# Mamba-2 scan and SwiGLU block on one core: row sums kept once with a negated selector, dummy products in five steps, roundings on other engines, and a new order of all steps

## The chip, the cores and the metric

The kernel runs on one core of a Trainium2 chip. A core has five instruction queues that work side by side: PE (matrix products, with PEld for the load of its weights), DVE (vector), ACT (activation functions), POOL (general) and SP, which here issues nearly all DMAs. The metric is the time of one execution on the device in microseconds (us). The runs of the kernel before gave 358.74 (median of three; 358.64, 358.74 and 359.39).

## The reference, cut to what matters

Two stages follow each other. The first is a Mamba-2 scan over 4 batches x 8 heads, 768 positions, 32 columns of x and 16 states, in chunks of 32. Its result, 3072 tokens x 256, goes through a SwiGLU block with 1536 hidden columns.

```python
log_a = np.log(np.clip(a, 1e-06, 1.0))
for c in range(nc):
    cum = np.cumsum(la, axis=-1)
    L = np.exp(cum[:, :, :, None] - cum[:, :, None, :]) * causal
    M = np.einsum('bhin,bhjn->bhij', Cc, Bc) * L
    y_intra = np.einsum('bhij,bhjd->bhid', M, xc)
    y_inter = np.einsum('bhin,bhnd->bhid', Cc, state) * np.exp(cum)[:, :, :, None]
    y[:, :, sl] = y_intra + y_inter
    Bx = np.einsum('bhjn,bhjd->bhjnd', Bc, xc) * np.exp(cum[:, :, -1:] - cum)[..., None, None]
    state = np.exp(np.sum(la, axis=-1))[:, :, None, None] * state + np.sum(Bx, axis=2)
...
x = attn_out.transpose(0, 2, 1, 3).reshape(B * S, H * D)
rms = np.sqrt(np.mean(x * x, axis=-1, keepdims=True) + 1e-06)
xn = x / rms * rms_g
g = xn @ w_gate
silu = g * (1.0 / (1.0 + np.exp(-g)))
return (silu * (xn @ w_val) @ w_out)
```

## The kernel before, in words

**Stages.** The 3072 tokens are six blocks of 512, and each block is two pairs of 256 tokens (pairs 0 to 11). A pair goes through the scan with chunks of 64 or 128 positions instead of 32; a finished block is normed and goes through the SwiGLU products. Block 0 has to pass the scan before any large product can run, so the start of the kernel is the scan of pairs 0 and 1 together with what must be set up for it. Later the scan of a block is interleaved with the products of the blocks before it.

**Large products.** A step `X.block.f.m` (`gv_split`, L1173) makes one 128 x 512 tile of the gate (m = 0) or the value (m = 1) for hidden columns f, as six products of 128 x 512: the operands are split into a high, a low and a mixed part (`xh`, `xl`, `xk` against `wh` and `wp`). `OX` (`o_split`, L1242 and L1248) multiplies the hidden parts `hh`, `hl`, `hk` with the output weights; `OY` (`product_apart`, L1220) does so for the last block; `F` (L1163) and `OF` are the same products with whole operands. The parts are made by ACT, DVE or POOL: `hH` is the rounding to the high part on ACT, `hHv` the same on DVE, `hL` and `hLp` the low part on DVE and on POOL (L1094), `xH`, `xL`, `xK` and `wH`, `wL`, `wM` likewise for the inputs and the weights. A letter p or v at the end of a step's name says that POOL or DVE does it.

**The start.** `a` comes in by a DMA and is turned by PE (`aT`, L454), clipped on DVE (`la0`, L465), and ACT takes its log (`la`). From it PE makes the chunk sums `c` (`chunk_sums`, L570 and L572), other sums `d` (L552 and L555) and, for the pairs 0 and 1, the row sums `r.0`, for the pairs 2 and 3 `r.1` (`sums_of_logs`, L525). `r.k` multiplies the logs with `mids`, a matrix of two halves: `mid` (a triangle about the middle, on POOL) and its negative (`minus_mid`, L485). DVE splits the result into three bf16 parts (`three_parts`, L536 to L541) and puts them into one tile `row` of 128 x 256, positive half and negative half. Then `mask.p.half` writes the causal mask into a bank of PSUM (L608, two products `whole16` x `ident16`), `sums.p.half` adds to it `row` against a selector `sel` (L622, eight small products) and `sel` against the negative half of `row` (L629, two products), and `exp` (ACT) makes the decays `L` of it. Before `r.1`, the step `middles` changes `mid` for chunks of 64 (POOL, L433 and L436, and again `minus_mid`). Other steps there: `turn.p` turns B and C of a pair (L704), `g` multiplies them (L771), `last` and `A`, `y` finish the pairs; `pow`, `man`, `wt` prepare the bf16 parts of the weights; `cx` and `cc` make `early` (ACT and POOL) and its column sums `fcol` (`chunk_column`, L586). `hmask`, `upto`, `after`, `never`, `ident`, `part`, `head`, `sel`, `mean` are constants that POOL and DVE make.

**Dummy products.** `warm` is a tile of zeros. `idle.n` (L447) multiplies it n times with itself into a bank that nobody reads, and `c*2` puts two such products (`filled`, L131) into the bank of `c` ahead of its real ones.

**What sets the order.** The order of the work is a text of steps, written out by hand, that the kernel walks through; there is no scheduler. Each engine executes its own instructions in the order in which the steps issue them. `i:` steps are kinds of the start, `p:` steps take a pair, `b:` steps a block. Banks of PSUM and places of SBUF are handed out by rings, first freed, first used, so the order also says which buffer a step gets. Every DMA goes out in this order from SP's queue, apart from half of the loads of the first pair, which go from ACT's; `fetch.k` loads piece k of the weights (511.5 KB), `bc.p` and `x.p` load B, C and x of a pair.

Of the kernel before, what the change touches and what calls it, by code (L numbers as in the profile page):

```python
# [9 lines left out]
FP32 = mybir.dt.float32  # L10
# [40 lines left out]
def kernel(  # L51
# [12 lines left out]
    nc = tc.nc  # L64
# [302 lines left out]
    mids = lead.tile([P, 2, P], FP32, name="mids")  # L367
# [10 lines left out]
    sel = const.tile([P, NH], BF16, name="sel")  # L378
    kinks = const.tile([P, 3], FP32, name="kinks")
# [6 lines left out]
    mid = mids[:, 0]  # L386
# [45 lines left out]
    def from_middles():  # L432
        nc.gpsimd.tensor_copy(out=mid, in_=upto)  # L433
        for r in halves:
            half_of = slice(r.start, r.start + HC // 2)
            nc.gpsimd.tensor_scalar(out=mid[half_of, r], in0=mid[half_of, r], scalar1=-1.0,  # L436
                                    scalar2=None, op0=ALU.add)
        minus_mid()
# [45 lines left out]
    def minus_mid():  # L484
        nc.gpsimd.tensor_scalar(out=mids[:, 1], in0=mid, scalar1=-1.0, scalar2=None,  # L485
                                op0=ALU.mult)

# [16 lines left out]
                                               op0=ALU.mult),  # L504
        "mid": from_middle, "middles": from_middles,
# [7 lines left out]
        "log": logs, "mids": minus_mid,  # L513
# [9 lines left out]
    def sums_of_logs(k):  # L523
        ps["r", k] = b, r_ps = bank((P, 2, P), 1, "r")
        nc.tensor.matmul(out=r_ps.rearrange("p s m -> p (s m)"),  # L525
                         lhsT=la4[k].rearrange("p q k h -> p (q k h)"),
                         rhs=mids.rearrange("p s m -> p (s m)"), start=True, stop=True)

    def three_parts(k):
        b, r_ps = ps.pop(("r", k))  # L530
        t = h.take(1, "parts")
        both = view(t, [P, 4, P], FP32)
        first = both[:, 0].bitcast(BF16).rearrange("p (s m) -> p s m", s=2)
        second = both[:, 1].bitcast(BF16).rearrange("p (s m) -> p s m", s=2)
        rest = both[:, 2:4]
# [4 lines left out]
        rows[k] = row = const.tile([P, 2, P], BF16, name="row%d" % k)  # L540
# [71 lines left out]
    def sums(p, half, e):  # L612
# [6 lines left out]
        for k, hd in enumerate(heads):  # L619
            for i, r in enumerate(rows_of):  # L620
                for u in parts:
                    nc.tensor.matmul(out=e[i][u, k * n:(k + 1) * n],  # L622
                                     lhsT=sel[r, hd:hd + 1].to_broadcast([32, n]),
                                     rhs=row[r, 0, u], start=p >= 2 and k == 0, stop=False,
                                     tile_position=(r.start, u.start), skip_group_check=True)
        hs = slice(heads[0], heads[-1] + 1)
        for i, r in enumerate(rows_of):
            for u in parts:
                nc.tensor.matmul(out=e[i][u], lhsT=row[r, 1, u],  # L629
                                 rhs=sel[r, hs].unsqueeze(2).to_broadcast([32, len(heads), n]),  # L630
# [714 lines left out]
    def token_out():  # L1345
# [82 lines left out]
        i:sums.1.1 i:exp.0.1 i:fetch.6 i:g.0.1 i:exp.1.1 i:sums.0.0 p:scale.1 p:Tt.1.1 i:last.1
        p:scale.0 p:T.1 i:r.1 i:g.0.0 i:exp.0.0 i:L.0.1 i:tok i:Tl.1 i:g.1.1 i:pow.2 i:mask.1.0
        i:parts.1 i:L.0.0 i:last.0 i:sums.1.0 i:A.1 i:exp.1.0 i:row.1 i:A.0 i:L.1.1 i:g.1.0 i:Tl.0  # L1430
        p:S.0 i:tokout p:bc.2 i:pow.0 i:fetch.1 i:y.0 i:rowe.1 p:bc.3 i:sq.0 i:row.0 i:limit i:L.1.0
        i:sums.3 p:S.1 i:man.0 i:pow.6 i:y.1 i:wt.0 i:rowout.1 i:yt.0 p:dT.2 i:fetch.4 p:turn.2
        i:sq.1 i:yt.1 i:early.0.0 i:open i:man.6 i:wt.6 i:man.1 i:fetch.5 i:man.2 i:exp.3 b:ms.0
        i:rowe.0 i:cav.3 i:early.0.1 i:pow.1 i:sums.2 i:wHv.6 i:wt.1 b:rs.0 i:wt.2 i:fetch.3 p:x.2
        p:dT.3 p:x.3 i:fetch.12 i:fetch.8 p:T.2 i:xn i:exp.2 p:Tt.2.1 p:turn.3 p:Td.2 i:early.1.0
        i:norm.0 p:Tt.2.0 p:T.3 p:Tt.3.1 i:wHv.2 i:rowout.0 i:man.4 i:early.1.1 b:F.0.2.0 i:pow.4
        p:scale.3 i:wt.4 p:Tt.3.0 i:norm.1 b:xH.0.1 i:pow.5 i:ca.2 b:gb.1 i:wL.6 b:L.1.1 b:F.0.4.0
        i:fetch.10 p:scalep.2 b:xH.0.0 b:silu.0.2 i:silu.0 b:xLp.0.1 i:pow.3 b:L.1.3 p:Td.3
        b:F.0.3.0 b:L.1.2 b:L.1.0 b:xK.0.1 b:xK.0.0 i:wHv.1 i:mana.3 b:xLp.0.0 p:A.2 p:S.2 p:A.3
        i:wt.3 b:silu.0.4 i:man.5 i:pow.12 b:F.0.5.0 i:wMp.6 b:X.0.7.0 b:X.0.6.0 i:wHv.3 p:S.3  # L1440
        p:qb.5 b:silu.0.5 i:wL.3 b:silu.0.3 i:fetch.9 i:pow.8 i:man.12 i:fetch.11 p:yi.2 i:wt.5
        p:ya.2 i:pow.10 b:silu.0.6 i:wM.3 p:yi.3 p:ya.3 i:fetch.13 i:wHv.5 b:sq.1.0 i:hid.0 i:wt.12
        p:qc.5 i:wL.5 b:X.0.2.1 i:silu.1 b:yt.1.1 i:mana.10 b:hid.0.2 i:gains i:mana.8 p:vB.5
        i:wMp.5 b:silu.0.7 i:wt.10 b:sq.1.1 b:X.0.3.1 i:fetch.7 i:wt.8 i:pow.13 i:man.13 b:yt.1.0
# [144 lines left out]
```

## Time and profile before

| what | value |
|---|---|
| time, median of three runs | 358.74 us (358.64 to 359.39) |
| span of the profiled execution, first to last instruction | 357.0 us |
| PE busy | 352.7 us (99%) |
| DVE busy | 283.5 us (79%) |
| ACT busy | 196.6 us (55%) |
| POOL busy | 91.1 us (26%) |
| mean granted clock of PE | 0.999 |

The profile gives the profiled execution's span only, not its own time; between the span and the median of the runs lie 1.74 us (358.74 - 357.0), which I take for what lies around the span. Rows of the timeline give start, duration, engine, line and tile; in square brackets stand idle time ahead of the first instruction and what ended it. Rows of the chain follow the end of the kernel back to its start, in order of time. Two instructions of PE can overlap, since it is pipelined: their starts tell more than their durations.

### The profile page before, as it was taken

How to read it: one execution, taken by the hardware profiler on the slowest of the kernel's cores; microseconds unless marked ns; L12 is line 12 of the kernel's file. 1: busy time of each engine (PE TensorE's matmuls, PEld its weight loads, DVE VectorE, ACT ScalarE, POOL GpSimd, SP SyncE). 2: the span in 40 equal slices, each digit the busy share in tenths (PEclk: the TensorE clock that was granted, in tenths of full speed). 3: DMA queues.
4: the chain of work that ended last, by engine and by line, in shares of the span. 5: the costliest groups of instructions: out<-in, count | busy, mean ns of one | idle time of the engine just before them, and what ended most of it. 6: DMA issues, size and time to landing. Idle time of an engine off the chain costs nothing.

```text
span 357.0 us, 8314 instructions
## 1 busy us (share of the span) xinstructions
PE 352.7 (99%) x3329; PEld 285.0 (80%) x3329; DVE 283.5 (79%) x507; ACT 196.6 (55%) x338; POOL 91.1 (26%) x91
## 2 busy tenths in 40 slices
PE   8999999999999999999999999999999999999996
PEld 5677578887888878878788788788788888888896
DVE  6899999999998999987887955877357582875791
ACT  3888999994756757494154672463345342112510
POOL 4125314256211326540123320025101111311000
PEclk9999999999999999999999999999999999999999
DMA  8978986672261345443123011200010021001003
GB/s 105 213 124 242 281 233 189 176 162 51 42 155 55 96 81 136 80 76 75 31 64 102 8 31 29 48 14 2 7 31 0 1 37 23 0 0 31 0 2 88
DMA packets 94556, 27.88 MB, mean 78 GB/s; under 512 B 77463, under 2 KB 92471, under 8 KB 94519
## 3 DMA queue, kind: packets, MB, share of 16 engines
q1 hardware_dynamic: 92438, 27.23, 33.4%
q8 instruction: 26, 0.43, 0.5%
q10 hardware_dynamic: 2080, 0.13, 0.4%
q14 instruction: 12, 0.09, 0.1%
HBM read 23.68 MB, written 3.67 MB: 77 GB/s over the span
## 4 chain that ended last, share of the span: by engine, by line
PE 98%; DVE 1%; issue 0%
PE gv L1173 53%; PE o L1242 19%; PE o L1248 8%; PE y L929 3%; PE o L1220 2%; PE gv L1163 2%; PE gv L1126 2%; PE g L778 2%; PE A L843 1%; PE g L771 1%; PE e L608 1%; PE y L904 1%; PE e L622 1%; PE ms L1027 0%; PE idle L447 0%; PE row L1311 0%
## 5 line engine op out<-in xcount | busy, mean ns | idle before, releaser
L1173 PE MATMUL gv<-xh,wh 128*128 128x512 f32 x272 | 87.0, 401 | 0.0
L272 ACT ACTIVATE hx<-gv 128x512 f32<-128x512 f32 x70 | 40.2, 595 | 80.2 <-PE gv L1173 36.7
L1173 PE MATMUL gv<-xl,wp 128*128 128x512 f32 x272 | 84.1, 390 | 0.0
L1173 PE MATMUL gv<-xk,wp 128*128 128x512 f32 x272 | 83.8, 390 | 0.0
L1096 DVE SCALAR_TENSOR_TENSOR hk<-hx,hh 128x512 fp32r<-128x512 f32 x65 | 53.0, 827 | 25.4 <-PE o L1242 18.9
L1094 POOL TENSOR_TENSOR hl<-hx,hh 128x512 fp32r<-128x512 f32 x21 | 29.7, 1418 | 131.1 <-DVE hk L1096 30.4
L1173 PEld LDWEIGHTS gv<-xl,wp 128*128 128x128 f32 x272 | 51.1, 188 | 11.0
L1173 PEld LDWEIGHTS gv<-xk,wp 128*128 128x128 f32 x272 | 51.1, 188 | 10.9
L1173 PEld LDWEIGHTS gv<-xh,wh 128*128 128x128 f32 x272 | 50.0, 188 | 10.8 <-issue 0.6
L1188 DVE SCALAR_TENSOR_TENSOR hx<-gv,hx 128x512 f32<-128x512 f32 x70 | 47.0, 684 | 13.4 <-PE gv L1173 12.4
L341 ACT ACTIVATE hh<-hx 128x512 fp32r<-128x512 f32 x37 | 22.8, 629 | 39.8 <-PE o L1242 11.9
L1242 PE MATMUL o<-hh,wh 128*128 128x512 f32 x96 | 37.9, 395 | 0.0
L1242 PE MATMUL o<-hl,wp 128*128 128x512 f32 x96 | 37.4, 390 | 0.0
L1242 PE MATMUL o<-hk,wp 128*128 128x512 f32 x96 | 37.4, 390 | 0.0
L1094 DVE TENSOR_TENSOR hl<-hx,hh 128x512 fp32r<-128x512 f32 x44 | 31.1, 721 | 2.8 <-PE o L1242 1.3
L266 ACT ACT_TABLE_LOAD x17 | 21.8, 1283 | 1.1 <-PEq L1573 0.8
L264 ACT ACT_TABLE_LOAD x17 | 21.8, 1283 | 0.3
L1242 PEld LDWEIGHTS o<-hh,wh 128*128 128x128 f32 x96 | 18.0, 188 | 4.2 <-issue 0.4
L336 POOL TENSOR_TENSOR wp<-wh,wp 128x512 fp32r<-128x512 f32 x9 | 13.0, 1449 | 32.6 <-DVE wp L328 25.0
L1242 PEld LDWEIGHTS o<-hk,wp 128*128 128x128 f32 x96 | 18.0, 188 | 3.8
L1242 PEld LDWEIGHTS o<-hl,wp 128*128 128x128 f32 x96 | 18.0, 188 | 3.6
L328 DVE SCALAR_TENSOR_TENSOR wp<-wh,w 128x512 fp32r<-128x512 f32 x27 | 19.6, 751 | 0.0
(184 smaller groups left out, 548.2 us busy)
## 6 DMA issues: line engine op xcount, KB each, us to landing
L<-rowd SPq DMA_DIRECT2D x32, 128.0 KB
x<-in_x_dram SPq DMA_DIRECT2D x24, 128.0 KB
wr<-in_moe_w_out_dram SPq DMA_DIRECT2D x6, 511.5 KB
wr<-in_moe_w_gate_dram SPq DMA_DIRECT2D x5, 511.5 KB
wr<-in_moe_w_val_dram SPq DMA_DIRECT2D x5, 511.5 KB
out_dram<-ob SPq DMA_DIRECT2D x28, 64.0 KB
bc<-in_B_dram SPq DMA_DIRECT2D x23, 64.0 KB
bc<-in_C_dram SPq DMA_DIRECT2D x23, 64.0 KB
```

Source lines behind the costliest of these rows:

```text
L264: nc.scalar.preload_act_table(AF.Silu)
L266: nc.scalar.preload_act_table_set("natural_log_exp_and_others")
L272: nc.scalar.activation(**operands)
L328: nc.vector.scalar_tensor_tensor(out=(low_parts, mixed_parts)[i][k], in0=high_parts[k], scalar=(-UP, GAIN)[i], in1=view(ws[k], shape), op0 ...
L336: nc.gpsimd.tensor_tensor(out=mixed_parts[k], in0=high_parts[k], in1=low_parts[k], op=ALU.subtract)
L341: nc.scalar.activation(out=out, in_=in_, func=AF.Copy, scale=scale)
L1094: engine.tensor_tensor(out=out, in0=v, in1=high, op=ALU.subtract)
L1096: nc.vector.scalar_tensor_tensor(out=out, in0=v, scalar=REST, in1=high, op0=ALU.mult, op1=ALU.subtract)
L1173: nc.tensor.matmul(out=o, lhsT=weights_of(m, t, f)[part], rhs=view(x, [P, TB], F32R), start=(part == t == 0), stop=(part == 2 and t == 1))
L1188: nc.vector.scalar_tensor_tensor(out=v, in0=o, scalar=gain(blk, f), in1=v, op0=ALU.mult, op1=ALU.mult)
L1242: nc.tensor.matmul(out=o, lhsT=w[:, b * P:(b + 1) * P], rhs=v, start=opens, stop=True, skip_group_check=True)
L1248: nc.tensor.matmul(out=o[:, j * DM:(j + 1) * DM], lhsT=v[:, tk], rhs=w, start=opens, stop=True, skip_group_check=True)
```

## The change

1. `mids` of 128 x 2 x 128 becomes `mid` of 128 x 128; the step that made its negative half is gone. `r.k` has 128 columns instead of 256, the split into three parts works on half the width, and `row` is 128 x 128. The second half of each sum takes the minus sign from a new constant, `minus` = -`sel` (128 x 8 bf16, DVE).
2. `fcol` is no longer one reduction on DVE but three additions on POOL, of widths 4, 2 and 1.
3. Dummy products: `idle.7` and `c*2` become `idle.2`, `idle.2`, `idle.2`, `idle.1`, `idle.1` and `idle.1`: nine before and nine after. `idle.2` stands ahead of `aT`, five dummies between `aT` and `c`, one behind `r.0`, one between two masks.
4. Roundings and others change engines. Counted over the text: `hH` on ACT 37 to 30, `hHv` on DVE 28 to 35; `hL` on DVE 44 to 40, `hLp` on POOL 21 to 25; parts of the weights on POOL 9 to 7 and on DVE 27 to 29; `Td` on DVE 8 to 4, on POOL 2 to 6; the scalings of pairs 0 and 1 go to POOL, subtractions on POOL go from 5 to 8.
5. All steps stand in a new order.

```diff
-    mids = lead.tile([P, 2, P], FP32, name="mids")
+    mid = lead.tile([P, P], FP32, name="mid")
...
+    minus = const.tile([P, NH], BF16, name="minus")
...
-        minus_mid()
...
+        "minus": lambda: nc.vector.tensor_scalar(out=minus, in0=sel, scalar1=-1.0, scalar2=None,
+                                                 op0=ALU.mult),
...
-        ps["r", k] = b, r_ps = bank((P, 2, P), 1, "r")
-        nc.tensor.matmul(out=r_ps.rearrange("p s m -> p (s m)"),
-                         lhsT=la4[k].rearrange("p q k h -> p (q k h)"),
-                         rhs=mids.rearrange("p s m -> p (s m)"), start=True, stop=True)
+        ps["r", k] = b, r_ps = bank((P, P), 1, "r")
+        nc.tensor.matmul(out=r_ps, lhsT=la4[k].rearrange("p q k h -> p (q k h)"), rhs=mid,
+                         start=True, stop=True)
...
-        rows[k] = row = const.tile([P, 2, P], BF16, name="row%d" % k)
+        rows[k] = row = const.tile([P, P], BF16, name="row%d" % k)
...
-        nc.vector.reduce_sum(out=fcol, in_=ps["fsel"], axis=AX.X)
+        rest = ps["fsel"]
+        for w in (4, 2, 1):
+            out = fcol.unsqueeze(2) if w == 1 else ps["full"][:, :, 4 - w:4]
+            nc.gpsimd.tensor_tensor(out=out, in0=rest[:, :, 0:w], in1=rest[:, :, w:2 * w],
+                                    op=ALU.add)
+            rest = out
...
-                                     rhs=row[r, 0, u], start=p >= 2 and k == 0, stop=False,
+                                     rhs=row[r, u], start=p >= 2 and k == 0, stop=False,
...
-                nc.tensor.matmul(out=e[i][u], lhsT=row[r, 1, u],
-                                 rhs=sel[r, hs].unsqueeze(2).to_broadcast([32, len(heads), n]),
+                nc.tensor.matmul(out=e[i][u], lhsT=row[r, u],
+                                 rhs=minus[r, hs].unsqueeze(2).to_broadcast([32, len(heads), n]),
...
-        i:warm i:a i:set i:bc.0 i:ident i:bc.1 i:bc2.1.1 i:ones i:zeros i:ident16 i:whole i:kinks
-        i:idle.7 i:after i:never i:fetch.2 i:whole16 i:mean i:part i:head i:part2 i:sel i:after2
...
+        i:ones i:hmask i:upto i:ident i:part i:warm i:idle.2 i:zeros i:a i:fetch.2 i:whole i:aT
+        i:la0 i:bc.0 i:mid i:idle.2 i:head i:set i:idle.2 i:log i:log4.0.4 i:idle.1 i:tmask
```

What the new order does to DVE and POOL at the very start. DVE before:

```order
L489 MEMSET warm 128x128
L494 MEMSET ones 128x128
L495 MEMSET never 128x128
L506 CAST ident_81<-ident 128x128
L403 MEMSET chunk_ones 128x256
L405 MEMSET chunk_ones 64x128 x2
```

and after:

```order
L489 MEMSET ones 128x128
L415 TENSOR_REDUCE part<-ident 128x4
L484 MEMSET warm 128x128
L490 MEMSET never 128x128
L403 MEMSET chunk_ones 128x256
L405 MEMSET chunk_ones 64x128 x2
L464 TENSOR_SCALAR early<-aT 128x64x3
```

`warm` was DVE's first instruction and is now behind `part`, which reads `ident`. POOL's, which makes `ident`, before:

```order
masks.py:197 MEMSET ident 128x128
masks.py:199 ISA
masks.py:199 AFFINE_SELECT ident<-ident 128x128
L399 AFFINE_SELECT after<-ones 128x128
L399 AFFINE_SELECT never<-never 128x128
L399 AFFINE_SELECT upto<-ones 128x128
```

and after:

```order
L408 ISA
L408 AFFINE_SELECT hmask<-ones 128x8
L410 AFFINE_SELECT hmask<-hmask 128x8
L399 AFFINE_SELECT upto<-ones 128x128
masks.py:197 MEMSET ident 128x128
masks.py:199 AFFINE_SELECT ident<-ident 128x128
```

`ident` moved behind `hmask` and `upto`, which read `ones`. PE from the chunk sums `c` to the first row sums, by name and number of the tiles, before:

```order
L570 MATMUL c_176<-la_80,chunk_ones_76 128x192 x2
L572 MATMUL c_176<-la_80,ones_72 128x32
L525 MATMUL r_185<-mids_77,la40_78 128x256
L704 MATMUL tp_189<-ident_71,bc_104 128x128 x4
L552 MATMUL d_194<-la_80,upto_73 128x192
L552 MATMUL d_194<-la_80,after_75 128x192
L555 MATMUL d_194<-la_80,ones_72 64x4x8 x2
L704 MATMUL tp_217<-ident_71,bc_113 128x128 x4
L622 LDWEIGHTS sel_89
L622 MATMUL e_165<-row0_211,sel_89 128x128
```

and after (`e_210` and `e_211` get their two masks here, and so do `e_222` and `e_223` behind a dummy):

```order
L565 MATMUL c_153<-la_80,chunk_ones_76 128x192 x2
L567 MATMUL c_153<-la_80,ones_72 128x32
L522 MATMUL r_157<-mid_77,la40_78 128x128
...
L704 MATMUL tp_192<-ident_71,bc_127 128x128 x4
L608 LDWEIGHTS ident16_81
L608 MATMUL e_210<-whole16_82,ident16_81 128x512
...
L522 MATMUL r_227<-mid_77,la41_79 128x128
L622 LDWEIGHTS sel_89
L622 MATMUL e_210<-row0_208,sel_89 128x128
```

The turn of the second pair (`bc_113` before) left this stretch, and four mask products and the second row sums, `r_227`, came in. Before, the masks of `e_165` and `e_166` (and of `e_150` and `e_151`) ran ahead of `c`. SP's queue, before:

```order
L392 DMA a_101<-in_a_dram 96x256
L160 DMA bc_104<-in_B_dram 128x8x16
L160 DMA bc_104<-in_C_dram 128x8x16
L160 DMA bc_113<-in_B_dram 128x8x16
```

and after:

```order
L392 DMA a_115<-in_a_dram 96x256
L241 DMA wr_117<-in_moe_w_gate_dram 128x2x1023
L160 DMA bc_127<-in_B_dram 128x8x16
L160 DMA bc_127<-in_C_dram 128x8x16
L241 DMA wr_147<-in_moe_w_gate_dram 128x2x1023
L160 DMA bc_160<-in_B_dram 128x8x16
```

Two weight pieces (`wr_117` and `wr_147`) came ahead of B and C of the second pair (`bc_160`, before `bc_113`).

More of the change, by code (lines that the diff above doesn't have):

```diff
@@ L482, in logs @@
         ps["early"].used()
-    def minus_mid():
-        nc.gpsimd.tensor_scalar(out=mids[:, 1], in0=mid, scalar1=-1.0, scalar2=None,
-                                op0=ALU.mult)
     settings = {
@@ L512 @@
         "idle": idle, "aT": turn_a, "la0": clipped, "log4": logs_again,
-        "log": logs, "mids": minus_mid,
+        "log": logs,
         "bc": lambda p: load(p, (nc.sync, nc.scalar) if p == 0 else (nc.sync,) * (1 if p == 1 else 2)),
@@ L531, in three_parts @@
         t = h.take(1, "parts")
[L532 to L535, printed above, removed]
+        both = view(t, [P, 2, P], FP32)
+        first, second = both[:, 0].bitcast(BF16)[:, 0:P], both[:, 0].bitcast(BF16)[:, P:2 * P]
+        rest = both[:, 1]
         nc.vector.tensor_copy(out=first, in_=r_ps)
@@ L1422 @@
     order = """
-        i:warm i:a i:set i:bc.0 i:ident i:bc.1 i:bc2.1.1 i:ones i:zeros i:ident16 i:whole i:kinks
-        i:idle.7 i:after i:never i:fetch.2 i:whole16 i:mean i:part i:head i:part2 i:sel i:after2
-        i:mask.0.0 i:upto i:mid i:upto2 i:eps i:aT i:la0 i:log i:mask.0.1 i:mids i:log4.0.4 i:hmask
-        p:x.1 i:c*2 p:x.0 i:r.0 i:cx p:turn.0 i:d i:tmask i:gcol i:log4.4.2 i:dx i:log4.6.2
-        i:fetch.0 i:parts.0 i:middles p:turn.1 p:Tt.1.0 i:sums.0.1 i:Tb.0 i:mask.1.1 i:cc p:T.0
@@ L1428 @@
[L1428 to L1444, printed above, removed]
-        b:sqav.1 p:spread.8 i:fetch.14 i:hid.1 i:fetch.17 i:pow.11 b:OF.0.0.1 b:X.0.5.1 b:X.0.4.1
@@ new lines @@
+        i:part2 i:log4.4.2 i:after i:idle.1 i:cx i:sel i:fetch.0 p:x.0 i:kinks i:after2 i:d
+        p:turn.0 i:man.2 p:x.1 i:eps i:minus i:parts.0 i:mask.0.1 i:middles i:idle.1 i:dx i:Tb.0
+        i:mask.1.1 p:T.0 i:r.1 i:sums.0.1 i:g.0.1 i:parts.1 i:pow.6 p:scalep.0 i:exp.0.1 i:gcol
+        i:last.0 p:turn.1 i:mask.0.0 i:Tl.0 i:sums.0.0 i:sums.1.1 i:L.0.1 i:g.0.0 p:Tt.1.0 p:T.1
+        i:man.6 p:Tt.1.1 i:mean p:scalep.1 i:last.1 i:exp.0.0 i:exp.1.1 i:mask.1.0 i:sums.1.0
+        i:L.0.0 i:Tl.1 i:g.1.1 i:g.1.0 i:limit i:wt.6 i:exp.1.0 i:A.0 i:pow.2 i:cc i:fetch.1
@@ new lines @@
+        i:row.1 i:L.1.1 p:S.0 i:tok i:pow.0 i:L.1.0 p:bc.3 i:rowe.1 i:A.1 i:rowout.1 p:S.1
+        i:mana.0 i:wt.0 i:y.0 p:bc.2 i:yt.0 i:tokout i:y.1 i:fetch.3 i:yt.1 i:sq.0 i:wt.2
+        i:sums.2 i:sq.1 i:sums.3 i:exp.3 i:pow.1 i:row.0 i:wH.6 i:gains i:fetch.4 i:man.1
+        i:early.0.0 i:wt.1 i:cav.3 p:x.3 i:rowe.0 b:ms.0 i:rowout.0 p:turn.3 b:rs.0 i:early.0.1
+        p:dT.2 i:early.1.0 p:scale.3 p:T.3 p:turn.2 i:xn i:exp.2 p:Tt.3.1 p:x.2 p:Tt.3.0
+        i:fetch.8 p:T.2 i:wHv.1 p:scalep.2 i:open i:ca.2 b:xH.0.0 i:norm.0 p:Tt.2.1 i:wL.6
```

227 lines of the change are left out of this document (121 added, 106 removed).

## The prediction

> **What bounds the kernel now.** I read the page first: busy times, the clock's row, and the shares of the chain that ended last.
>
> ```profile
> span 357.0 us, 8314 instructions
> PE 352.7 (99%) x3329; PEld 285.0 (80%) x3329; DVE 283.5 (79%) x507; ACT 196.6 (55%) x338; POOL 91.1 (26%) x91
> PEclk9999999999999999999999999999999999999999
> PE 98%; DVE 1%; issue 0%
> ```
>
> PE is busy 352.7 of 357.0 us and carries 98% of the chain. Next, what PE waited for, by the list of waits for PE alone; it has a single row.
>
> ```profile
> PE idle L447 <- DVE warm L489: 1.1, 1, 1.1
> ```
>
> Apart from its first product, which waits until DVE has cleared `warm`, no wait of PE is long enough to be listed. So three things move the time: when PE starts, what it executes and at which clock, and new waits. Then the chain of waits over the first 12 us, in order of time (start, us, what).
>
> ```profile
> 0.90 0.18 DVE warm L489
> 1.12 1.67 PE idle L447 x7
> ...
> 4.09 0.85 PE e L608 x2
> 4.94 0.32 PE c L131 x2
> 5.26 0.86 PE c L570 x4
> ...
> 6.27 0.53 PE r L525 x2
> ...
> 8.76 0.40 PE e L622 x8
> 9.16 0.21 PE e L629 x2
> 9.37 0.54 PE e L608 x2
> ...
> 10.92 0.40 PE g L771 x4
> 11.32 0.37 PE last L756 x2
> ```
>
> Although the page's coarse clock row shows full speed throughout, the same pair of L608 products takes 0.85 at 4.09 and 0.54 at 9.37. A dummy of L447 takes 1.67/7 = 0.24; two of the same shape at 4.94 take 0.32, not 0.48. They fit half speed for 0.16 and full speed after, so the clock is released at about 4.94 + 0.16 = 5.10, which is 3.98 after the first product at 1.12.
>
> [...]
>
> **The change part by part.** My landmark is the first row-sum product (L622, at 8.76): its place in PE's order is comparable in both, and up to it the two orders differ most. First its forerun, by the timeline.
>
> ```profile
> 0.80 0.20 POOL masks.py:197 MEMSET ident<- 128x128 f32 x1 [0.29 <-POOLq L1573]
> 1.08 0.29 POOL masks.py:199 TENSOR_SCALAR_AFFINE_SELECT ident<-ident 128x128 f32<-128x128 f32 x1
> ...
> 1.82 0.28 POOL L399 TENSOR_SCALAR_AFFINE_SELECT upto<-ones 128x128 f32<-128x128 f32 x1
> 2.77 0.23 DVE L415 TENSOR_REDUCE part<-ident 128x4 f32<-128x128 f32 x1
> 2.91 0.37 DVE L426 TENSOR_REDUCE head<-ident 128x8 f32<-128x128 f32 x1
> 3.57 0.52 PE L454 MATMUL aT<-ident,a 96*128 96x96 f32 x2
> 4.28 0.48 DVE L465 TENSOR_SCALAR early<-aT 128x192 f32<-128x192 f32 x1
> 4.79 0.56 ACT L272 ACTIVATE la<-early 128x192 f32<-128x192 f32 x2 [2.71 <-DVE early L465]
> 4.86 0.19 POOL L408 TENSOR_SCALAR_AFFINE_SELECT hmask<-ones 128x8 f32<-128x8 f32 x1
> 5.12 0.19 POOL L410 TENSOR_SCALAR_AFFINE_SELECT hmask<-hmask 128x8 f32<-128x8 f32 x1
> 5.21 0.92 PE L570 MATMUL c<-la,chunk_ones 128*128 128x192 f32 x4
> ```
>
> *PE's start.* `warm` is now cleared behind `part` on DVE, and `part` reads `ident`, which POOL now makes behind three selects. From 1.12, the time by which `ones` can be ready (it goes first, as `warm` did): two hmask selects 0.26 each (4.86 to 5.12), `upto` 0.28, the clearing of ident 0.28 (0.80 to 1.08), its select 0.29: 2.49. Then `part`, 0.14 until the next step can go (2.77 to 2.91) and at most its own 0.23, and from DVE's clearing to PE's first product 0.22 (0.90 to 1.12): 2.85 to 2.94. I take 2.87, near the low end, as DVE's steps overlap like that all along these rows. PE starts 1.75 later.
>
> *The chunk sums c.* In its place: two dummies 0.48 end at 3.35, aT 0.52, the clip 0.04 behind it, and as before 0.51 from the clip to the log (4.28 to 4.79) and 0.42 from the log to c (4.79 to 5.21): 4.84 instead of 5.21, **-0.37**. It comes from four L608 products that no longer run ahead of c. The five dummies between aT and c fill time in which PE waits for the log anyway.
>
> *PE's work from c to the landmark.* Rows for its parts:
>
> ```profile
> 6.10 0.68 PE L525 MATMUL r<-mids,la 128*128 128x256 f32 x2
> 6.62 0.60 PE L704 MATMUL tp<-ident,bc 128*128 128x128 f32 x4
> 7.05 0.49 PE L552 MATMUL d<-la,upto 128*128 128x192 f32 x2
> ...
> 8.04 0.66 PE L704 MATMUL tp<-ident,bc 128*128 128x128 f32 x4
> ```
>
> Before: 8.76 - 5.21 = 3.55. After, at full speed: c 0.89 (from its start at 5.21 to r's at 6.10); the first r at half width 0.26 (half of 6.10 to 6.62); d 0.99 (7.05 to 8.04); one turn 0.43 (6.62 to 7.05); four masks 0.90 (twice 0.85/2, and a little for the start); the second r 0.35 (the same 0.26, and 0.09 because it stands between products of another shape); two dummies 0.22 (0.24 each at half speed). Sum 4.04: **+0.49**. Most of this is work fetched forward: the other turn and its masks come later, so turn 0.44 + mask 0.54 stand there instead of mask 0.54 + r 0.53, **-0.09** (the chain's rows at 9.37 and 6.27).
>
> *The clock.* If the release follows the first product by 3.98 again, it comes at 2.87 + 3.98 = 6.85, and c and what follows run from 4.84 to 6.85 at half speed. Before, c began after the release. Loss: (6.85 - 4.84)/2 = **+1.00**. This is the largest term and the least sure; the bounds are 0 (released by 4.84) and, with a release 1.75 later still, +1.88.
>
> [...] The rows here know only the one lag.
>
> *A wait of the second r.* It stands ahead of the row sums now and needs `middles` from POOL. POOL's rows:
>
> ```profile
> 6.97 1.06 POOL L580 TENSOR_TENSOR early<-early,hmask 128x416 f32<-128x416 f32 x1 [1.67 <-ACT la L272]
> 7.98 0.35 POOL L433 COPY mids<-upto 128x128 f32<-128x128 f32 x1
> 8.42 0.94 POOL L436 TENSOR_SCALAR mids<-mids 32x64 f32<-32x64 f32 x2
> ```
>
> They end at 9.36, 3.09 after c's products (the chain's r begins at 6.27). At half speed c ends at 4.84 + 2 x 0.89 = 6.62, or 0.17 later if its last results take as long to come out as here (6.10 to 6.27), so `middles` is there at 9.71 to 9.88. PE would come to r at 4.84 + 1.00 + 4.04 - 0.35 = 9.53: a wait of 0.18 to 0.35, **+0.20**, near the low end because the selects and copies ahead may begin sooner on a POOL with nothing else to do. Behind r wait all row sums. With the clock released early the wait is nothing, so the bounds are 0 and 0.35. The dropped negations (one POOL step for each r) and the halved three-part split on DVE (from 1.9 us at 6.82 to 8.72) lie beside PE's turns and masks: no saving on the path.
>
> *Switches.* Between full-array products and short or tiled ones PE loses a little. Around one place in the middle:
>
> ```profile
> 250.41 0.61 PE L1173 MATMUL gv<-xk,wp 128*128 128x512 f32 x2
> 250.95 0.43 PE L1027 MATMUL ms<-sq,mean 128*32 128x128 f32 x8
> 251.31 0.73 PE L1173 MATMUL gv<-xh,wh 128*128 128x512 f32 x2
> ```
>
> A pair usually follows the last after 0.45; here 0.54 passes, and the first pair behind takes 0.73 instead of 0.61. One stretch costs 0.09 going in and 0.12 coming out. In PE's order I count 27 stretches of full-array products before and 23 after: three fewer in the start (at 0.09) and one later (at 0.2), **-0.47**, between 0 and -0.8.
>
> *Roundings on other engines.* A rounded part costs twice as much on POOL as on DVE:
>
> ```profile
> L1094 POOL TENSOR_TENSOR hl<-hx,hh 128x512 fp32r<-128x512 f32 x21 | 29.7, 1418 | 131.1 <-DVE hk L1096 30.4
> L1094 DVE TENSOR_TENSOR hl<-hx,hh 128x512 fp32r<-128x512 f32 x44 | 31.1, 721 | 2.8 <-PE o L1242 1.3
> ```
>
> Four move to POOL (+5.7 us there, -2.9 on DVE), seven high parts go from ACT to DVE, scalings and subtractions go to POOL, and the column sum `fcol` becomes three POOL additions. I cost all of it at nothing. The cover is PE's list of waits: with these engines busy 79, 55 and 26% of the span, PE never waits for them. If a rounding comes late anywhere, the next O or X product waits, at most the 1.42 of one POOL rounding a time. `minus` (128x8) is one small DVE step like `sel`, ahead of its first reader by the whole split.
>
> *DMA.* SP now issues two weight pieces of 511.5 KB ahead of the second pair's B and C. Later in the kernel the transfers reach this rate:
>
> ```profile
> 25.00:45.00 20.00, 20.00 (x286) 12.91 (x287) 19.82 (x43) 18.52 (x32) 8.06 (x6) 1.00 0.91 250
> ```
>
> At 250 GB/s a piece takes 2.05. The second turn ran at 8.04 before, so B and C were there by then; two pieces more make 12.1 at worst. PE comes to that turn at 9.9 + 0.61 (row sums, 0.40 + 0.21) + 0.40 (four g) + 0.37 (last) = 11.3, so between 0 and +0.8 is lost. I take 0, as 8.04 is only when PE got there, and keep 0.8 as a rival.
>
> Sum: -0.37 + 0.49 - 0.09 + 1.00 + 0.20 - 0.47 = **+0.76**. The profiled span of 357.0 and what lies around it make the median of 358.74 (1.74 outside), so the forecast is 358.74 + 0.76 = 359.5. A measurement of this kernel can tell 0.2%, 0.72 us, from no change; the forecast lies on that edge.
>
> **The rivals.**
> - *The clock is released as early as before*, by 4.84 or so: the term of 1.00 goes, and the wait for `middles` with it, since c ends sooner: 358.74 - 0.44 = 358.3 (0.76 - 1.00 - 0.20). For it: the one release seen need not follow the first product. Against: no product at all runs before 2.87.
> - *The release comes later still (slower).* The mechanism is the same, with a lag up to 1.75 longer: +0.88 more, 360.3. It decides from a release at about 6.9. For it: the runs of before spread from 358.64 to 359.39, 0.75 us, as a release that moves by 1.5 us would make them. [...]
> - *The second turn waits for B and C* behind two weight pieces: +0.6 beside the forecast, 360.1. It decides where they land after 11.3. For it: the queues are 0.9 busy when in full use. Against: the turn stood 3 us earlier before.
> - *The order gains in its switches (faster)*: if all four stretches cost their full 0.21 or more, the release is early and no wait appears: -0.37 + 0.49 - 0.09 - 0.84 = -0.81, 357.9. Against: only a pair of rows speaks for the price.
>
> **How the numbers follow.** Forecast 0.35, early release 0.20, later release 0.18, the turn's wait 0.14, the faster order 0.11, something else within 0.2% 0.02. Faster takes the last rival and a quarter of the early release: 0.16. Slower takes half of the forecast (it lies on the edge), nearly all of the later release and two thirds of the turn's wait: 0.44. The rest, 0.40, is within 0.2%. The range reaches from 358.2 (leaves out the faster order and the low end of the early release) to 360.8 (later release and the turn's wait together lie above); the forecast's own is 358.9 to 360.0.
>
> **What would show it.** In the profile after: the first dummy near 2.9 and c near 4.8; a pair of L608 products or a c at twice its full-speed time up to about 6.9; the second r released by POOL near 9.7; the row sums near 10; no row of PE waits for ACT, DVE or POOL after 13 us. The prediction is wrong if a dummy starts near 1.1, if the products from c on run at full speed, or if PE's list shows waits in the middle. Then the roundings were not covered.

## The result, and the profile after

The changed kernel takes 362.78 us (median of four; 362.76 to 363.92), 1.0108 times the kernel before, with an interval of 1.009 to 1.0126: 3.8 us slower than the kernel before in the same set of runs (358.94), where 359.5 and a range up to 360.8 were forecast. The profiled execution is one of 362.78 with a span of 361.1, so 4.1 of span are to be found. The page after, in the lines that were shown of before:

```profile
span 361.1 us, 8297 instructions
...
PE 352.5 (98%) x3329; PEld 286.6 (79%) x3329; DVE 279.0 (77%) x500; ACT 198.2 (55%) x337; POOL 101.3 (28%) x102
...
PEclk9999989999999999999999999999999999999999
...
PE 95%; DVE 2%; issue 1%; ACT 1%; POOL 0%; POOLq 0%; DVEq 0%
```

PE has the same number of products and the same busy time; one digit of the clock's row is an 8, in the sixth of 40 slices, at 45 to 54 us. The list of PE's waits (us in total, times, longest) has a second row now:

```profile
PE idle L446 <- DVE warm L484: 2.9, 1, 2.9
PE y L929 <- issue: 2.6, 1, 2.6
```

"issue" is a wait for nothing that the profile shows: no semaphore, no buffer, no engine. Where it lies, by the chain of after (start, us, what):

```profile
38.83 0.72 PE A L843 x47
39.55 1.91 PE gv L1163 x4
41.46 1.10 PE y L929 x72
42.56 2.57 issue
45.13 1.46 PE y L929 x77
46.59 11.01 PE gv L1173 x42
```

and the same place in the chain of before:

```profile
38.87 0.72 PE A L843 x49
39.59 1.91 PE gv L1163 x4
41.51 2.75 PE gv L1173 x12
44.25 2.38 PE y L929 x160
46.63 1.59 PE gv L1173 x6
```

Up to 41.5 us the two profiles are level (A at 38.83 and 38.87): all that the change did to the start has come to nothing by then. Then before runs twelve X products and the y products of block 1 (184 small ones, each a weight load and a product, in 2.4 us); after begins the y products at once and stops in their middle for 2.57 us. What follows is slow too. By stretches (us, PE's busy time and instructions, granted clock, share of the DMA engines, GB/s):

```profile
41.00:42.56 1.56, 1.56 (x99) 1.00 1.03 387
42.56:45.13 2.57, 0.00 (x1) 1.00 1.05 389
...
46.00:49.00 3.00, 3.00 (x39) 0.50 0.47 77
```

From 46 to 49 the clock is at half. The 42 X products from 46.59 take 11.01 where seven groups of six at 1.375 (2.75 for two of them in the chain of before) take 9.6: 1.4 lost. Gap 2.57 and clock 1.4 are 4.0 of the 4.1 us.

### The profile page after: what moved, and what is told of

The parts are those of the page before. It is cut to its first block, busy times and chain, and to the rows that moved or that the text cites. A ratio compares the mean times of both kernels' runs of the same rounds, so it can differ in the third digit from the quotient of the medians.

```text
span 361.1 us, 8297 instructions
## 1 busy us (share of the span) xinstructions
PE 352.5 (98%) x3329; PEld 286.6 (79%) x3329; DVE 279.0 (77%) x500; ACT 198.2 (55%) x337; POOL 101.3 (28%) x102
## 4 chain that ended last, share of the span: by engine, by line
PE 95%; DVE 2%; issue 1%; ACT 1%; POOL 0%; POOLq 0%; DVEq 0%
PE gv L1173 52%; PE o L1242 18%; PE o L1248 8%; PE y L929 3%; PE o L1220 2%; PE gv L1163 2%; PE gv L1126 2%; PE g L778 2%; PE A L843 1%; DVE L L811 1%; PE idle L446 1%; PE tp L704 1%; PE ms L1027 0%; PE c L565 0%; DVE w L312 0%
## 5 line engine op out<-in xcount | busy, mean ns | idle before, releaser
L1094 POOL TENSOR_TENSOR hl<-hx,hh 128x512 fp32r<-128x512 f32 x25 | 36.0, 1444 | 120.9 <-PE o L1242 65.6
L341 ACT ACTIVATE hh<-hx 128x512 fp32r<-128x512 f32 x30 | 18.7, 628 | 29.5 <-PE o L1242 12.0
L1094 DVE TENSOR_TENSOR hl<-hx,hh 128x512 fp32r<-128x512 f32 x40 | 28.5, 721 | 2.8 <-PE gv L1173 1.5
L644 POOL TENSOR_SCALAR_AFFINE_SELECT L<-L 64x512 f32<-64x512 f32 (+1 forms) x18 | 16.9, 938 | 17.5 <-ACT L L272 16.8
L344 DVE TENSOR_SCALAR hh<-hx 128x512 fp32r<-128x512 f32 x35 | 18.6, 541 | 3.9 <-PE o L1242 3.8
```

Of the source, the lines that this page charges most:

```text
L341: nc.scalar.activation(out=out, in_=in_, func=AF.Copy, scale=scale)
L344: nc.vector.tensor_scalar(out=out, in0=in_, scalar1=scale, scalar2=None, op0=ALU.mult)
L644: nc.gpsimd.affine_select(out=L[r], in_=L[r], pattern=[[0, L.shape[1]], [1, HC]], compare_op=ALU.is_ge, fill=0.0, base=0, channel_multipli ...
L1094: engine.tensor_tensor(out=out, in0=v, in1=high, op=ALU.subtract)
```

## The experiments

**Theory A** says that PE ran out of instructions. The page counts loads of instructions in queues of their own, and one of them fits PE:

```profile
q8 instruction: 26, 0.43, 0.5%
```

26 loads for PE's 2 x 3329 instructions make 256 each, 16 KB in one packet. While the y products run, PE uses up 184 x 2 = 368 in 2.4 us. In the gap the DMA engines are full of data, and a load of instructions is among them (the queues' rows for 42.6 to 45.1 us of after):

```profile
q1 hardware_dynamic: 528, 0.96, 102.2%
...
q8 instruction: 1, 0.02, 2.6%
```

When a load is asked for stands in no trace; the times and counts of that in the expectations (about the 1000th instruction, at 39.4 us) are the author's estimate. The load before it came, in the same profile, after 719 products and weight loads (30.51 us), and 256 more make 975, which PE reached at 39.2.

The rivals: **B**, the y products wait for an operand or a buffer that the profile does not name; **C**, the loss comes from the start after all.

**X products first.**

```diff
-  p:A.3 b:F.0.5.0 p:S.3 ... p:ya.2 ... p:S.2 ... p:yi.3 p:yi.2 b:xK.0.1 b:X.0.7.0 ... b:silu.0.5
+  p:A.3 b:xK.0.1 b:F.0.5.0 p:S.3 ... p:S.2 b:X.0.7.0 b:silu.0.5 b:X.0.6.0 p:ya.2 ... p:yi.3 p:yi.2
```

> The changed kernel with 12 of its X products (steps X.0.7.0 and X.0.6.0, with the steps that they need) put ahead of the y products of block 1, so that PE is busy for 2.7 us with few instructions before the 184 small ones. Theory A (PE ran out of instructions: the load of its next 256 was asked for at about its 1000th instruction, at 39.4 us, and came in 2.6 us too late for the stream of y products): the gap of 2.57 us is gone or below 0.3 us, the clock stays full after it, and the time is 358.5 to 359.2, as before the change. Theory B (the y products waited for an operand or a buffer that the profile does not name): the gap remains, moved behind the X products and shortened by their 2.7 us at most if the operand comes at 45.1 whatever PE does, but then it would be gone as well; B differs by a named releaser or a gap anywhere else. Theory C (the loss lies in the start, not here): 362 to 363.

360.70, 1.0053 (1.0041 to 1.0065): 2.1 us better than the change as it is. The gap fell to 0.14 (chain, at 46.13) and the clock stayed up, as A says; C is out for these 2.1 us. But 1.9 over before remained, and PE's list had a new row:

```profile
PE gv L1163 <- DVE u L1139: 1.2, 1, 1.2
```

**Two weight loads over the y products.**

```diff
-  i:fetch.12 i:fetch.11 p:ya.2 ... p:yi.2
+  p:ya.2 ... p:yi.2 i:fetch.12 i:fetch.11
```

> The changed kernel with two weight loads of 511.5 KB (pieces 12 and 11) issued behind the y products instead of ahead of them; PE's order is the same. Theory A, if the load of instructions stands in the DMA engines behind data: the instruction load starts 1 to 2 us sooner after the same number of PE instructions, the gap shrinks from 2.57 to between 0 and 1.6 us, the time is 358.7 to 361.5. Theory B: gap of 2.57 and 362.8, since no operand of y comes with these pieces. If the load's delay has nothing to do with the traffic, also 362.8.

363.68, 1.0125 (1.0107 to 1.0142), gap 3.1. This edit tested nothing: between the old and the new place stand only steps of other engines, so SP's own order of loads stayed the same. Its use is as a repeat of the changed kernel, in which the wait of 1.2 for DVE came up as well; five runs took from 362.09 to 364.35.

**The kernel before, y products first.**

```diff
-  b:X.0.7.0 b:X.0.6.0 i:wHv.3 p:S.3 ... p:yi.2 i:wt.5 p:ya.2 i:pow.10 b:silu.0.6 i:wM.3 p:yi.3 p:ya.3
+  i:wHv.3 p:S.3 ... p:yi.2 i:wt.5 p:ya.2 i:pow.10 i:wM.3 p:yi.3 p:ya.3 b:X.0.7.0 b:X.0.6.0 b:silu.0.6
```

> The kernel before with its 12 X products put behind the y products of block 1, nothing else changed: the reverse of the first edit. Theory A: PE stops in the middle of the y products after about 1220 instructions, as in the changed kernel, for 1 to 3 us, the clock falls to half for some 3 us after it, and the time is 361 to 363. Theory B: the y products find their operands as before or wait with a named releaser; 358.7 to 359.5. If the order of steps in the first 23 us is the cause, nothing happens here.

360.60, 1.0060 (1.0042 to 1.0078). In the timeline the y products stop twice:

```profile
43.59 0.27 PE L929 MATMUL y<-T,S 32*64 32x64 f32 x1 [0.55 <-DVE S L869]
44.46 0.46 PE L929 MATMUL y<-T,S 32*64 32x64 f32 x23 [0.61 <-issue]
```

First for `S`, which DVE has not finished so early, and then, one product later, for "issue". The direction is A's, the size was over-estimated: the wait for `S` covered part of the load's delay, and in this profile the clock stayed up. So the median missed its range. Two of the six runs had a granted clock of 0.994 to 0.995 and took 361.79 and 362.20, the others 359.97 to 360.65.

**The row-sum part alone.**

```diff
-  i:sel i:after2 ... i:mids          (mids 128 x 2 x 128)
+  i:sel i:minus i:after2 ...         (mid 128 x 128, row 128 x 128, minus = -sel)
```

> The kernel before with the row-sum part of the change alone: 128 columns, one bf16 row, the constant minus made on DVE behind sel; the order is the old one. If the two row-sum products lie on PE's path they save 0.26 each at full speed: 358.2 to 358.7. If the first of them only fills time in which the row sums wait for the split on DVE (which is halved, 1.9 to some 1.3 us), the row sums come 0.5 sooner or, where PE's turns fill that time, nothing changes: 358.6 to 359.0.

359.18, 1.0010 (1.0002 to 1.0019). A miss of both forecasts: no gain, if anything 0.4 lost. The last experiment goes on from here.

**Three weight loads behind B and C of pair 4, in SP's queue.**

```diff
-  i:fetch.12 i:fetch.11 p:ya.2 ... i:fetch.14 p:qc.4
+  p:ya.2 ... p:qc.4 i:fetch.12 i:fetch.11 i:fetch.14
```

> The changed kernel with three weight loads of 511.5 KB (pieces 12, 11 and 14) put behind the loads of B and C of pair 4 in SP's queue, so that they go out at about 47 us, after the y products; PE's order is the same. (The earlier edit that moved two of them over the y products left SP's own order as it was, since only PE's steps stood between, and so tested nothing.) Theory A with the DMA engines as the cause: the load of PE's instructions starts within 2 us of being asked for (3.3 before), the gap of 2.57 falls to 0 to 1.2, the clock stays up, the time is 358.7 to 361. If the load is late for another reason: gap 2 to 3 and 362 to 364.

362.97, 1.0123 (1.0108 to 1.0138). In the profile (an execution of 361.51, the best of four) the gap is 1.4, by PE's list of waits:

```profile
PE y L929 <- issue: 1.4, 1, 1.4
```

and by stretches of 1 us (columns as above):

```profile
42.00:43.00 1.00, 1.00 (x67) 1.00 0.55 65
43.00:44.00 1.00, 0.79 (x53) 1.00 0.12 29
```

The DMA engines empty at 42 us, and the gap halves without vanishing. Counted from the start of the A products, the load's packet comes after 3.1 us (42.84, A at 39.76) where it came after 3.8 in after (42.67, A at 38.83); PE goes on 2.4 or 2.5 us behind the packet in both (45.24, 45.13). So taking the three loads out of the way is worth some 0.7 of the 2.6 us; the rest of the difference is mostly that the products ahead of the stop took 1.39 instead of 1.10. Full DMA engines alone are not the measure: in the kernel before they were as full (103.5% from 38 to 42 us), and the packet came 2.8 us after A began (41.66, A at 38.87). The other three runs had a lower clock as well (0.994 to 0.995) and took 362.9 to 363.8, so the median lies where the forecast put a load that is late for another reason. What makes it late is shown in part only.

**100 more instructions of PE at the start.**

```diff
+    def tick(n):
+        b, v = bank((P, 256), 1, "idle")
+        for k in range(n):
+            nc.tensor.matmul(out=v[:, 0:16], lhsT=warm[0:32, 0:P], rhs=warm[0:32, 0:16],
+                             start=True, stop=True, tile_position=(0, 0), skip_group_check=True)
+        b.used()
...
+  i:warm i:ones ... i:idle.2 i:tick.50 ...
```

> The changed kernel with warm cleared first on DVE and 50 products of 16 columns (100 instructions of PE, each a weight load and a product) put behind the first two dummies, in time in which PE has nothing else to do. Theory A: all loads of instructions shift by 100 instructions against the work. The load that came too late is asked for at the old 885th instead of the 985th instruction, in the F products at about 36 us, and is there in time; the next is asked for in the middle of the y products, at about 42 us, and PE runs dry at the old 1373rd instruction, 9 products before the last of the 184 y products, for 1.5 to 4 us. So the gap stands at the end of the y products and no longer behind the 98th. Theory B (an operand): the gap stays behind the 98th y product. Time 360.5 to 364.

375.72, 1.0456 (1.043 to 1.0481), far slower than expected. The profiled execution took 380.13 at a granted clock of 0.973, so only the places in it are read here and not its durations. The first row is of the changed kernel, the others of this one:

```profile
41.39 1.17 PE L929 MATMUL y<-L,x 64*32 64x64 f32 x97
...
45.67 1.48 PE L937 MATMUL y<-L,x 64*32 64x64 f32 x128
47.08 0.80 PE L937 MATMUL y<-T,S 32*64 32x64 f32 x47
52.67 0.50 PE L937 MATMUL y<-T,S 32*64 32x64 f32 x9 [4.79 <-issue]
```

PE stops after 128 + 47 = 175 of the 184 y products, 9 before the last, exactly where the count of instructions put it; in the changed kernel it stopped after 97. No operand can do that: the operands are the same. The list of waits shows five such gaps now:

```profile
PE y L937 <- issue: 10.8, 5, 4.8
```

The shift that moved one gap brought four more, in the y products of later blocks. With PE's semaphore instructions counted in, the five stops come after 1473, 2497, 3521, 4545 and 5569 of its recorded instructions, each 1024 = 4 x 256 behind the last. Counting products and weight loads in the traces, PE stopped after 1197 of them in five kernels (the changed one, the second, third and fifth experiment, and the next), and after 1197 + 256 = 1453 at the first stop of this one. The third experiment has the steps of the kernel before; the number is the same. This is what makes A shown and not argued.

**`warm` first.**

```diff
-  i:ones i:hmask i:upto i:ident i:part i:warm i:idle.2
+  i:warm i:ones i:hmask i:upto i:ident i:part i:idle.2
```

> The changed kernel with warm cleared first on DVE, as before the change; nothing else. The first product runs at 1.1 instead of 2.86, the chunk sums still start at 4.8 to 4.9, and if the clock's release follows the first product they run at full speed; before, they ran at half speed to about 8.2. The first row sums come at 9.1 to 9.4 instead of 10.58 (the second r then waits for POOL). If the work up to 23 us is bound by ACT and DVE behind them, only part of that arrives, 0.3 to 1.2 us. The gap at the y products stays behind the 98th; if the load of instructions comes when the weight loads ahead of it are done, it grows by what was won, and the time stays at 362 to 363; otherwise 361.5 to 362.5.

363.97, 1.0148 (1.0124 to 1.0173). The first product ran at 1.1, but c started at 4.73 and still at half speed; the clock came up at 9.0, by its records. Between its first product and c PE had a pause of 1.37, because `aT` came at 3.1 when `a` had landed. The row sums came at 10.8, no sooner than the 10.64 of after, and the gap was 2.57 again. The median lies 1.2 above the changed kernel's and outside both ranges; the profiled execution is the fastest of the four, 362.95, so what the others lost is not shown.

```profile
PE aT L453 <- DMA a<-in_a_dram: 1.4, 1, 1.4
```

**Both, X products and `warm` first.** The edits of the first experiment and of the one just above together.

> The changed kernel with 12 X products ahead of the y products (as in the first experiment, which took 360.70) and warm cleared first. If the start's half clock costs what is seen at the row sums (1.3 to 1.6 us), 359.1 to 359.4; if the work behind is bound by ACT and DVE, 359.8 to 360.7. If the loads of instructions are then late again by what was won, 360.7.

360.69, 1.0052 (1.0040 to 1.0065): the first experiment's time. But the row sums came at 10.74, in the first experiment's profile at 9.98: `warm` first did not bring the work forward, so this run does not say what an earlier start would be worth.

**Weights behind the norm.** The wait of 1.2 us that the first experiment brought to light. Rows of the timeline of that experiment (POOL and DVE):

```profile
28.89 2.82 POOL L644 TENSOR_SCALAR_AFFINE_SELECT L<-L 64x1024 f32<-64x1024 f32 x2 [0.88 <-ACT L L272]
...
29.36 1.36 DVE L344 TENSOR_SCALAR wh<-w 128x512 fp32r<-128x512 f32 x1
...
31.83 1.80 DVE L328 SCALAR_TENSOR_TENSOR wp<-wh,w 128x512 fp32r<-128x512 f32 x1
```

and of the changed kernel:

```profile
29.34 3.88 POOL L644 TENSOR_SCALAR_AFFINE_SELECT L<-L 64x1024 f32<-64x1024 f32 x2 [2.01 <-ACT L L272]
...
30.01 0.41 DVE L344 TENSOR_SCALAR wh<-w 128x512 fp32r<-128x512 f32 x1
...
31.55 0.67 DVE L328 SCALAR_TENSOR_TENSOR wp<-wh,w 128x512 fp32r<-128x512 f32 x1
```

The same instructions in the same order: in the one DVE is held up by 2.1 us, in the other POOL's two selects take 1.1 longer. It looks as if `wh` waited for a select of POOL in the one: half of POOL's 2.82, one select, ends at 30.30, and `wh` ends 0.42 later, at 30.72, as if it had begun then.

```diff
-  i:wHv.1 p:scalep.2 ... i:norm.0 p:Tt.2.1 i:wL.6 i:early.1.1 p:dT.3 i:norm.1
+  p:scalep.2 ... i:norm.0 p:Tt.2.1 i:early.1.1 p:dT.3 i:norm.1 i:wHv.1 i:wL.6
```

> The first experiment (12 X products ahead of the y products) with two DVE steps of the weights, wHv.1 and wL.6, behind the second half of the norm instead of ahead of it and between its halves. In that experiment's profile they took 1.36 and 1.80 us beside POOL's two selects (L644) and its rounding (L1094), where the changed kernel's profile has 0.41 and 0.67, and the first F product waited 1.2 us for DVE's u behind them. If that is the rest of the loss: the wait is gone and the time is 359.3 to 359.8 (360.70 - 1.2). If u itself is then stretched by POOL in their stead: 360.3 to 361.

361.05, 1.0058 (1.0045 to 1.0071): a miss. `u` was on time, and the next F product waited just as long for what DVE does after it:

```profile
PE gv L1163 <- DVE w L312: 1.2, 1, 1.2
```

DVE is busy for 11.62 of the 12 us from 28 to 40 there, so the order of its steps hardly matters; whether what it loses to POOL does is for the experiment after the next.

**The clock early.**

```diff
-  i:ones i:hmask i:upto i:ident i:part i:warm i:idle.2 ... (two more i:idle.1 behind r.0 and a mask)
+  i:warm i:ones i:hmask i:upto i:ident i:part i:idle.8 ...
```

> The ninth kernel with warm first on DVE and eight dummies in a row instead of two at the start (two single dummies further on are left out). Two dummies and then a pause until aT at 3.1 left the clock at half speed to about 9 us in the kernel with warm first; if what releases it is PE being busy without a pause from 1.1 on, the release comes at about 5 as before the change, c, d and the masks run at full speed, and the first row sums come at 9.0 to 9.5 instead of 10.8. The time is then 0.5 to 1.3 below the ninth kernel's, 358.2 to 359.2, or equal to it if ACT and DVE set the pace to 23 us.

360.98, 1.0055 (1.0041 to 1.0068): equal to the ninth, and the clock was not early.

```profile
1.12 1.89 PE L446 MATMUL idle<-warm 128*128 128x256 bf16 x8 [1.12 <-DVE warm L484]
3.46 0.55 PE L453 MATMUL aT<-ident,a 96*128 96x96 f32 x2 [0.45 <-POOL never L399]
...
4.99 1.65 PE L565 MATMUL c<-la,chunk_ones 128*128 128x192 f32 x4
...
9.79 1.03 PE L608 MATMUL e<-whole,ident 128*128 128x512 bf16 x4
```

c takes 1.65 (0.92 before); only the masks at 9.79 run at full speed. With a pause of 0.45 before `aT`, two microseconds of dummies did not bring the release forward.

**No selects on POOL.** Left out of the first experiment's kernel: step `i:ca.2`.

> The first experiment (12 X products ahead of the y products, 360.70) without the two selects that POOL runs over the decays of pair 2 (step ca.2, L644): this leaves out the causal mask of that pair, all else is computed. If POOL's selects stretch DVE's wh and wp (1.36 and 1.80 us beside them, 0.41 and 0.67 in the changed kernel's profile), and DVE, which is busy without a pause from 28 to 40 us, hands that on to the first F products: wh 0.4 and wp 0.7, PE's wait of 1.2 us for DVE is gone, 359.3 to 359.8. If DVE's own work is too much there whoever runs beside it: the wait stays above 0.8 and the time at 360.3 to 361.

359.43 (median of twelve, 358.79 to 360.28), 1.0014 (1.0004 to 1.0024): 1.27 better than the first experiment. The wait is gone, and the two DVE steps are short:

```profile
30.16 0.41 DVE L344 TENSOR_SCALAR wh<-w 128x512 fp32r<-128x512 f32 x1
...
31.69 0.67 DVE L328 SCALAR_TENSOR_TENSOR wp<-wh,w 128x512 fp32r<-128x512 f32 x1
```

So POOL's selects beside DVE are the price, and not DVE's own work. Of the 0.63 that remain over before (358.80 in the same set), PE's list has 0.3 for DVE's `w` and 0.2 for "issue"; the rest is open.

**The row-sum part alone, `minus` later.**

```diff
-  i:sel i:minus i:after2 ... i:aT i:la0 i:log
+  i:sel i:after2 ... i:aT i:la0 i:minus i:log
```

> The kernel before with the row-sum part of the change alone, as in the fourth experiment (359.18), but minus made on DVE behind the clip of a instead of ahead of it. There the clip began at 4.49 instead of 4.28 and c at 5.6 instead of 5.21. If that delay was the price: c at 5.2 again and 358.6 to 358.9, no change. If halving the row sums itself costs or wins on PE's path, the time stays at 359.2 or falls to 358.3.

359.16, 1.0015 (1.0004 to 1.0026): the place of `minus` was not the cause. In this profile the turn of pair 1, at 8.63 where it ran at 8.04 before, waits for the DMA of B:

```profile
PE tp L699 <- DMA bc<-in_B_dram: 0.5, 1, 0.5
```

With the shorter r, PE comes to the turn sooner, and B is not there. In the fourth experiment's profile the same turn takes 1.14 where before took 0.66. Why B lands later than 8.04, with the same DMAs ahead of it, stays open. Halving the row sums buys nothing here in any case.

None of these kernels beats the one before. The nearest are the row-sum part alone (1.0010) and the kernel without the selects, which leaves work out (1.0014).

## Why the prediction was wrong, point by point

**What bounds the kernel.** "So three things move the time: when PE starts, what it executes and at which clock, and new waits" held, but the new waits were looked for among data, buffers and DMAs of data. The step that failed is that every other new wait was put at nothing, with PE's list of waits of before as the cover ("PE never waits for them"): that list names waits that before had, and the stream of PE's own instructions, which is behind none of its rows, was not among the things that a new order can make late. Nothing in the sum stood for it: gap 2.57 and half clock 1.4 are 4.0 of the 4.1 us, and what stops PE is shown by the gap's place (1197, and 1453 with 100 instructions more). The prediction's own sign of being wrong, waits in the middle of PE's list, came true, but not for the reason it gave ("Then the roundings were not covered").

What could have been read of it before: the page has the queue of instructions with its 26 loads, and in before twelve X products, 2.75 us with few instructions, stand between A and the y products. In the rows of PE's order the change takes just this stretch away, and the short products follow A with only four long ones between.

**PE's start and c.** First product 2.86 (2.87 forecast), c at 4.88 (4.84). This part of the working was right to 0.04 (the chain, which begins a step where the one before it ends, has c at 4.97).

**The clock.** c took 1.56 in the chain of after where it took 0.86 before:

```profile
2.86 0.61 PE idle L446 x2
...
4.97 1.56 PE c L565 x4
...
10.64 0.22 PE e L622 x4
```

The timeline narrows the release down. The products of `d` come in two pairs, which took 0.49 each before:

```profile
7.39 0.85 PE L547 MATMUL d<-la,upto 128*128 128x192 f32 x2
8.03 0.60 PE L547 MATMUL d<-la,after 128*128 128x192 f32 x2
```

The first pair is at half speed, the second in part: the release lies at about 8.25, which is 5.4 after the first product and not the forecast 3.98. So the row sums came at 10.64 instead of the 10.1 that the terms made (4.84 + 1.00 + 4.04 + 0.20). But this lag is one draw. The profile of the second experiment has the same steps up to there, and in it the last two products of c run at full speed at 6.07 (0.30, where after has 0.47 at 6.32):

```profile
6.07 0.30 PE L567 MATMUL c<-la,ones 128*128 128x32 f32 x2
...
9.67 0.28 PE L622 MATMUL e<-row,sel 32*128 32x128 bf16 x4
```

The clock records in the traces give the times themselves: 8.25 in after, 5.90 in the second experiment, 6.98 in the first (row sums at 9.98), and 5.02 in before. The start of before moves as well: in the third experiment, which shares it, the first part of c took 1.24 where the profile of before has 0.92. So a lag taken from one profile could not be carried over, and the rival of a later release was right, in the one execution that was profiled.

Its price of 1.9 us at the landmark was not on the path in any case: 12.6 us later, at the first product of the early weights, the changed kernel was ahead.

```profile
23.26 1.92 PE gv L1126 x8
```

Before, the chain has that at 23.44. In the profiles of the first and second experiment, with row sums 0.6 and 0.9 sooner than in after, that product (by the timeline, 23.19 in after) comes at 22.72 and 22.85. So a sooner release was worth 0.3 to 0.5 there, and both then waited the 1.2 us for DVE. The step that failed here is "My landmark is the first row-sum product": the sum stops there, as if both orders needed the same from it on but for the terms named. It took 14.7 us from there before (8.76 to 23.44) and 12.6 after (10.64 to 23.26), with PE busy for 14.68 and 12.57 us of it, and with more products in after (288 against 253). The term for switches, -0.47 for the whole kernel, is mis-sized, since it took one price from a place in the middle, and the same small products did not cost the same in both orders. The 32 products of `g` took this in this stretch (us busy behind the bar, mean ns of one; first before, then after):

```profile
L771 PE MATMUL g<-T 32*128 32x256 f32 x32 | 4.6, 394 | 0.0
L771 PE MATMUL g<-T 32*128 32x256 f32 x32 | 3.4, 387 | 0.0
```

So 1.2 of the 2.1 us are theirs by this count. Which of the neighbours make the difference was not tried. In all, +0.76 for the start came out as about 0 in the profile of after (-0.2), since the loss at the landmark and the gain behind it cancelled: that they did was luck.

**The wait of the second r.** Forecast 0.18 to 0.35 for POOL; the list of after has no such row. With its later release `middles` was there in time; in the second experiment, where the release came sooner, r.1 starts 0.18 later behind the masks than in the first (9.25, 0.61 after the mask of 8.64, where the first has 0.43). So the wait is real, and small.

**The roundings, costed at nothing.** In the changed kernel's profile they cost nothing. But in the order of after PE waits 1.2 us for DVE in some executions, as in the second and fifth experiment, and 1.27 us went with two selects of POOL. The one run of 363.92 lies 1.15 above its fellows; whether that is this wait was not profiled. The prediction took the times of each engine as its own. The runs show that those of DVE and POOL are not independent there: `wh` and `wp` took 1.36 and 1.80 beside POOL's selects and the rounding behind them, and 0.41 and 0.67 with the selects left out; in the changed kernel's profile they took 0.41 and 0.67 as well, and there the selects took 3.88 instead of 2.82. Why they are not is in no trace.

**DMA.** The second turn ran in the chain of after behind `last` without a listed wait; the rival of a late B and C did not come about in this profile. In the second experiment's, PE came to that turn at 11.09, and its four products took 1.17 instead of 0.60; the view of that tile has 0.4 us of waiting for the DMA of B and 0.2 for that of C. So the rival's mechanism is real, with about its price of 0.6 there, and the late clock of after hid it.

**The rivals.** The early release did not come, the later one came but was not on the path, and the turn did not wait in after. The order's gain was real, but it lies behind the landmark. None named a late instruction. The range was wrong for want of a case, not for narrow bounds.

## What to carry to other kernels

A stretch of many short products can starve PE of its own instructions, as 184 products with as many weight loads, 2.4 us of work, did here for 2.57 us: count them from the start, in this case in blocks of 256, and keep a stretch of long products ahead of it. A gap of PE can cost more than itself: here the clock was at half for 3 us behind one of 2.57. Before a term for lost time at the start is added up, look for the place further on where both orders must come together, and ask which engine sets the pace up to there. Where the clock's release stands in the sum, take its lag from several executions: without a pause of PE it lay between 3.0 and 5.4 us here.

## What the runs showed of the hardware that was not expected

- PE stopped after the same number of products and weight loads (1197) in five kernels, one of them with the steps of before, and one load of instructions (256) later in the kernel that starts with 100 more. So what stops it is the count of its own instructions. The trace of before has its 26 loads too, and no such wait; in the changed kernel one load cost 2.57 us.
- Gaps of 0.61 us (third experiment) and 1.4 (fifth) left the clock up in those profiles; behind gaps of 2.57 (changed kernel) and 3.1 (second) it was at half for some 3 us.
- The clock's release is no fixed time behind the first product. By the clock records, with the same steps and no pause of PE, it came 3.0 (second experiment), 4.1 (first) and 5.4 us (after) behind it, and 3.9 in before. With a pause it came later than any of these: 7.9 and 8.5 us behind the first product in the two kernels whose PE starts at 1.1 and then stands still, for 1.37 (`warm` first) or 0.45 (the clock early).
- How soon a load of PE's instructions comes differs: its packet came 3.8 us after A began in the changed kernel, 3.1 with three weight loads put behind it, and 2.8 in before. From the packet to PE's next product 2.2 to 2.6 us passed in each gap of the first, second, third and fifth experiment and of the changed kernel. In the kernel before the packet came at 41.66, and 2.5 us later, at 44.2, PE was only beginning its y products (44.25).
